# Attention and a gated dense layer on one core: the opening and the main part as one table of steps, laid out anew

## The chip, the cores and the metric

One core of one Trainium2 chip. The metric is the device time of one execution in microseconds (us), as the median of several runs. The engines by the profile's names: PE (TensorE: matmuls; PEld are its weight loads), DVE (VectorE), ACT (ScalarE), POOL (GpSimd, which here also issues all loads) and SP (SyncE, which issues the stores).

## The reference

```python
scores = scale * np.matmul(q, k.transpose(0, 1, 3, 2)) - np.log(S)
attn = 1.0 / (1.0 + np.exp(-scores))
x = np.matmul(attn, v)              # then to [3584, 768]
h = x @ w_in
g = h * (1.0 / (1.0 + np.exp(-beta * h)))
return g @ w_out
```

q, k and v are 8 batches x 12 heads x 448 tokens x 64; w_in is 768 x 2048, w_out 2048 x 768, beta has one value for each of the 2048 columns. Inputs and output are float32.

## The kernel before, in words

All matmuls take fp16 operands; loads cast while they transfer (POOL's queue). Work goes by batches of 448 tokens (8), groups of four heads (24, three to a batch, numbered through) and slots of two heads. Output tiles have 128 tokens (28).

One group goes through these steps. `transpose` (L194, DVE, step R) turns q or k of a group. `visit` (L243, V g.jt) computes a part of the scores by matmuls on 32 rows of PE (L221) and evicts them with a sigmoid on ACT (`weigh`, L230, tile attnT). `attend` (L282, A g) multiplies by v on tiles of 128 rows and 64 columns (L294), the last part of the keys on 64 rows, and DVE casts the result into xT (L303).

The dense layers come next. All of their matmuls go through `dense` (L171): either one matmul with 128 columns of weights, or two of 64 columns beside each other, as `tiled["cols"]` says. For the first batch, and some columns of the second, `dense1` (L308, step D) is the plain product with w_in, a sigmoid on ACT (L320) and a product on DVE (L323) into gt; `dense2` (L341, step O) is the plain product with w_out. All later batches use a Strassen-Winograd scheme with 7 products in place of 8: `wino1` (I b.d.p) and `wino2` (U tile.p.part), with sums of weights (S, T), of tokens (X) and of hidden values (H), which DVE adds (`add`, L375); the second halves of the gating are `weigh_right` (L495, G) and `weigh_below` (L505, B) on POOL.

Matmul results go to one-bank tiles of PSUM from `bank()` (L89), which takes the one used longest ago; scores have two-bank tiles of their own. `share_psum` (L76) lays PSUM out anew once, when the opening's first part is through, and `scores_done` (L634) once the last visit is through.

Sizes of pools that matter: outp has 4 buffers ("osb", 128 x 896 floats). They hold some early attnT tiles, then the scratch a and b of each wino1 block, and the output tiles until `store` (L593, DMA issue at L605, SP's queue) has written them. rawp has 3 buffers for q and k as loaded; xTp has 3.

Every engine works in the order in which the program issues. That order is written out by hand: `STEPS` (L653 to L709) is a list of steps such as `V3.1` or `I2.3.2`, and `follow` (L641) runs them one by one. For each step it looks up which comes next, a V or an A (L646): if it is an A, dense matmuls ahead run as two of 64 columns (L648), else as one of 128.

Ahead of `STEPS`, the opening is plain code (L779 to L834). It computes the first three groups by halves of the tokens, 224 each: `half_visit` (L259), `attend` with 224 columns, and `first_half` (L610), which takes the next of sixteen half `dense1` steps. `idle_units` (L740) are matmuls on zeros that fill time at the start. The loads of q, k, v, w_in (`load_w_in`, L154, eight parts) and w_out (`load_w_out`, L161, four parts) are issued in this code too, all on POOL's queue. In the opening `tiled["cols"]` is 128 throughout. Here is its end:

```python
        firsts.close()
        share_psum(ctx, seconds, 2, N_ONE, 2)
        first_half(4)
        half_visit(1, QH, 0)
        first_half(3)
        half_visit(1, QH, 1)
        transpose(2, 0, NH, NB)
        attend(0, QH, QH)
        ...
        attend(2, QH, QH)
        first_half(1)
        follow(STEPS)
```

Of the kernel before, what the change touches and what calls it, by code (L numbers as in the profile page):

```python
# [13 lines left out]
def kernel(  # L14
# [638 lines left out]
    STEPS = """  # L653
        R3.1 R3.0 D0.6 D0.12 R4.1 D0.14 D0.7 V3.1 R4.0 D0.13 D0.0 D0.8 V3.0 D0.3 D0.9 V3.3 D0.1
        D0.10 E1 D0.2 Q6 V3.2 D0.4 O0.0.0 D0.5 O0.0.1 O0.0.2 V4.1 O1.0.0 O0.0.3 A3 V4.0 O1.0.1 R5.1
        D0.11 D0.15 O0.0.4 R5.0 V4.2 O0.0.5 S1.1 O0.0.6 O1.0.2 O1.0.3 S1.0 O0.0.7 S2.0 O1.0.4 V4.3
# [8 lines left out]
        I2.0.2 H4.1 I2.0.3 R10.1 X2.2 U4.1.0 V9.0 X2.3 U4.1.1 Q11 G2.0 U4.6.0 U4.6.1 Q12 A9 V10.0
        I2.0.7 H4.3 U4.5.0 U4.7.0 U4.5.1 V10.1 U4.7.1 I2.0.4 B2.0.1 U4.3.0 U4.4.0 U4.2.0 B2.0.0
        U4.2.1 R11.0 U4.3.1 U4.4.1 R11.1 I2.1.1 V10.2 Q13 Q14 I2.1.6 I2.1.5 I2.1.7 I2.1.2 K4 I2.1.3
        V10.3 I2.1.4 G2.1 B2.1.0 R12.1 I2.2.1 B2.1.1 A10 V11.0 I2.2.6 I2.2.5 R12.0 I2.2.7 I2.2.2
        I2.2.3 I2.3.1 Q15 G2.2 V11.1 I2.3.6 I2.2.4 B2.2.1 B2.2.0 I2.3.5 I2.3.2 R13.1 I2.3.7 I2.3.3
        V11.2 I2.3.4 B2.3.1 U6.1.0 B2.3.0 H6.2 U6.1.1 A11 H6.0 V12.2 U6.2.0 U6.7.0 H6.1 U6.2.1 G2.3  # L670
# [24 lines left out]
        I6.0.4 H18.3 U18.5.0 G6.0 U18.2.0 R23.0 U18.5.1 U18.2.1 B6.0.1 B6.0.0 U18.7.1 V22.3 U18.3.0
        U18.3.1 U18.4.0 U18.4.1 I6.1.1 I6.1.6 A22 V23.0 I6.1.5 I6.1.7 I6.1.2 I6.1.3 I6.2.1 G6.1
        I6.1.4 B6.1.0 I6.2.6 I6.2.5 B6.1.1 I6.2.2 V23.1 I6.2.7 I6.2.3 I6.3.1 I6.2.4 I6.3.6 G6.2
        B6.2.1 I6.3.5 B6.2.0 I6.3.7 I6.3.2 I6.3.3 V23.2 I6.3.4 B6.3.1 U20.1.0 H20.2 U20.1.1 A23
        U20.7.0 B6.3.0 U22.1.0 H20.0 U20.2.0 H20.1 X7.0 U20.2.1 U20.5.0 U20.6.0 G6.3 U20.6.1 I7.0.1
        U20.5.1 H20.3 X7.2 U22.1.1 U20.7.1 I7.0.2 X7.1 U20.3.0 U20.3.1 U22.2.0 U22.2.1 H22.0 U20.4.0  # L700
        X7.3 H22.2 H22.1 U20.4.1 U22.5.0 I7.0.6 I7.0.5 U22.7.0 I7.0.7 I7.0.3 U22.6.0 G7.0 I7.0.4
        I7.1.1 I7.1.6 I7.1.5 B7.0.0 B7.0.1 I7.1.2 I7.1.7 I7.2.1 I7.1.3 I7.2.6 G7.1 I7.1.4 I7.2.5
        I7.2.7 B7.1.0 B7.1.1 U22.6.1 I7.2.2 I7.2.3 U22.5.1 H22.3 I7.2.4 I7.3.1 I7.3.6 B7.2.0 I7.3.5
        G7.2 B7.2.1 I7.3.7 U22.7.1 I7.3.2 I7.3.3 U24.1.0 I7.3.4 U22.3.0 U22.3.1 U24.1.1 U22.4.0
        B7.3.0 U22.4.1 U24.2.0 B7.3.1 H24.0 U26.1.0 U24.2.1 H24.1 U24.5.0 G7.3 U24.6.0 H24.2 U24.6.1
        U24.5.1 H24.3 H26.0 U24.7.0 U24.7.1 U26.1.1 U24.3.0 U24.3.1 H26.1 U24.4.0 U26.2.1 U26.5.0
        U26.6.0 H26.2 U26.6.1 U26.5.1 H26.3 U26.7.0 U26.7.1 U24.4.1 U26.3.0 U26.3.1 U26.4.0 U26.4.1
        U26.2.0
# [7 lines left out]
    with tc.manual_schedule():  # L716
# [62 lines left out]
        for g in range(1, QPB):  # L779
            load_one(g, 0, 0, NH)  # L780
            load_one(g, 1)
        load_v(0)
# [1 line left out]
        for g in range(QPB - 1):
            load_one(g, 0, NH, NB)
        for c in range(WCH):
            if c == WCH // 2:
                load_one(QPB - 1, 0, NH, NB)
            load_w_in(c)
        for g in range(1, QPB):  # L790
            transpose(g, 0, 0, NH)
            transpose(g, 1)

        for n in range(2 * QPB):
            half_visit(n // 2, 0, n % 2)
            idle_units((3, 4, 4, 4, 2, 2)[n])
        double_v_last(0)
        transpose(0, 0, NH, NB)
        attend(0, 0, QH)
        half_visit(0, QH, 0)  # L800
        attend(1, 0, QH)
        half_visit(0, QH, 1)
        for g in range(1, QPB - 1):
            transpose(g, 0, NH, NB)
        attend(2, 0, QH, (0,))
        attend(2, 0, QH, (1,))
        for i in range(P // BLK):
            part = slice(i * BLK, (i + 1) * BLK)
# [57 lines left out]
```

## Time and profile before

| what | value |
|---|---|
| runs | 368.91, 369.24, 913.54 us; median 369.24 |
| span of the profiled execution | 367.57 us (page: 367.6) |
| median less span | 1.67 us |
| TensorE busy | 361.6 us, 3677 matmuls |
| granted clock of TensorE | 0.99 to 1.00 over the stretches of the span |
| chain by line | matmuls of `dense` 71%, scores 12%, values 10%, stores 2% |

The chain is followed back from the last instruction to what released each; its shares are of the span. In the busy time by stretch each engine has its busy us and, in brackets, its instructions. In the timeline and the chain the first number is the start in us from the span's start, the second the length; neighbours of one kind stand together with their number (x16). A name such as `m_ps<-xT,w_in 128*64 128x224` means: written tile, read tiles, tile of PE (rows*columns), size of the operand.

### The profile page before, as it was taken

What the parts mean: (1) busy time and instruction counts of PE and PEld (TensorE: products, weight loads), DVE (VectorE), ACT (ScalarE), POOL (GpSimd) and SP (SyncE); (2) the same over time, 40 slices, a digit from 0 to 9 for tenths busy, and PEclk for the clock granted to TensorE, in tenths of its full rate; (3) what the DMA queues carried; (4) which work ended last, traced back from release to release, by engine and by line L of the source; (5) the groups of instructions that cost most, each with busy time, mean ns of one, the idle gap of its engine ahead of it and who ended that gap; (6) DMA issues with size and microseconds to landing.
All of it is one profiled execution on the core that took longest, in us unless ns stands there. A gap on an engine that the chain in (4) does not pass through costs nothing.

```text
span 367.6 us, 9130 instructions
## 1 busy us (share of the span) xinstructions
PE 361.6 (98%) x3677; PEld 237.7 (65%) x3677; DVE 272.2 (74%) x524; ACT 248.7 (68%) x410; POOL 154.3 (42%) x192
## 2 busy tenths in 40 slices
PE   8999999999999999999999999999999999999996
PEld 3478754457465685557757667666856688689763
DVE  4356569889995796876778678868879677778764
ACT  5987976789765797657865579977874859225410
POOL 7834523504413873117761445841630316216610
PEclk9999999999999999999999999999999999999999
DMA  8999999930363890517909363373303030030233
GB/s 163 182 197 201 197 206 199 237 40 2 50 139 52 165 147 2 81 57 122 143 9 153 52 137 51 50 79 88 52 1 88 2 87 2 0 87 0 61 67 134
DMA packets 42698, 34.76 MB, mean 95 GB/s; under 512 B 21904, under 2 KB 39200, under 8 KB 42656
## 3 DMA queue, kind: packets, MB, share of 16 engines
q0 software_dynamic: 36688, 22.47, 44.7%
q1 hardware_dynamic: 5968, 11.71, 11.5%
q8 instruction: 29, 0.48, 0.6%
q14 instruction: 13, 0.11, 0.1%
HBM read 45.62 MB, written 11.01 MB: 154 GB/s over the span
## 4 chain that ended last, share of the span: by engine, by line
PE 94%; DMA 3%; ACT 1%; DVE 1%; SPq 0%; issue 0%; ACTq 0%; DVEq 0%
PE m_ps L174 71%; PE sco L221 12%; PE av_ps L294 10%; DMA out_dram<-osb 2%; PE idle_ps L743 1%; ACT attnT L233 1%; DMA gt<-in_k_dram 1%; DVE osb L375 0%; SPq L605 0%; ACT osb L428 0%; DVE xT L303 0%; ACT osb L466 0%; DVE raw L760 0%; SPq L726 0%; DVE kT L763 0%
## 5 line engine op out<-in xcount | busy, mean ns | idle before, releaser
L233 ACT ACTIVATE attnT<-sco 128x896 f16<-128x896 f32 (+1 forms) x163 | 139.2, 908 | 38.5 <-PE sco L221 37.9
L375 DVE TENSOR_TENSOR osb<-m_ps,osb 128x448 f32<-128x448 f32 (+2 forms) x197 | 116.3, 596 | 51.7 <-PE m_ps L174 42.2
L174 PEld LDWEIGHTS <-w_in 128*128 128x128 f16 (+1 forms) x948 | 81.0, 100 | 19.4 <-issue 11.5
L174 PE MATMUL m_ps<-xT,w_in 128*128 128x224 f16 (+3 forms) x750 | 85.5, 266 | 0.8 <-ACT osb L466 0.5
L495 POOL TENSOR_TENSOR gt<-osb,sg 128x448 f16<-128x448 f32 x26 | 29.5, 1135 | 118.4 <-ACT sg L428 108.2
L505 POOL TENSOR_TENSOR gt<-osb,sg 128x448 f16<-128x448 f32 x52 | 58.3, 1137 | 34.9 <-ACT sg L428 33.2
L428 ACT ACTIVATE sg<-osb,beta_sb 128x224 f32<-128x224 f32 (+1 forms) x104 | 54.0, 575 | 10.0 <-DVE osb L375 9.8
L174 PEld LDWEIGHTS <-sum 128*128 128x128 f16 (+1 forms) x444 | 39.9, 99 | 27.4 <-issue 3.7
L174 PEld LDWEIGHTS <-gt 128*128 128x128 f16 (+1 forms) x474 | 36.9, 102 | 25.8 <-issue 7.7
L174 PE MATMUL m_ps<-w_out,gt 128*128 128x384 f16 (+2 forms) x350 | 52.6, 324 | 0.0
L221 PE MATMUL sco<-qT,kT 32*128 32x448 f16 (+3 forms) x864 | 51.4, 340 | 0.4 <-DVE kT L763 0.2
L174 PEld LDWEIGHTS <-w_S 128*128 128x128 f16 (+1 forms) x486 | 43.9, 99 | 7.0 <-issue 6.0
L174 PE MATMUL m_ps<-w_out,sum 128*128 128x384 f16 (+1 forms) x228 | 40.6, 327 | 0.0
L174 PE MATMUL m_ps<-w_T,sum 128*128 128x384 f16 (+1 forms) x216 | 40.3, 326 | 0.0
L303 DVE CAST xT<-av_ps 128x448 f16<-128x448 f32 (+1 forms) x54 | 28.4, 566 | 14.3 <-PE av_ps L294 14.1
L294 PE MATMUL av_ps<-attnT,v 128*64 128x448 f16 (+3 forms) x400 | 38.2, 343 | 0.0
L174 PE MATMUL m_ps<-xs,w_S 128*128 128x224 f16 (+1 forms) x330 | 36.2, 259 | 0.0
L294 PEld LDWEIGHTS <-v 128*64 128x64 f16 (+1 forms) x432 | 20.5, 108 | 18.1 <-issue 10.2
L428 ACT ACTIVATE osb<-m_ps,beta_sb 128x224 f32<-128x224 f32 x52 | 20.4, 449 | 15.3 <-PE m_ps L174 13.8
L221 PEld LDWEIGHTS <-kT 32*128 32x128 f16 (+1 forms) x864 | 13.4, 96 | 23.1 <-issue 20.9
L466 ACT COPY osb<-m_ps 128x448 f32<-128x448 f32 x26 | 13.8, 536 | 18.4 <-PE m_ps L174 15.4
L135 POOL DMA_DIRECT2D v<-in_v_dram x32 | 19.9, 633 | 13.3 <-DMA w_out<-in_moe_w_out_dram 6.5
(53 smaller groups left out, 300.5 us busy)
## 6 DMA issues: line engine op xcount, KB each, us to landing
out_dram<-osb SPq DMA_DIRECT2D x100, 96.0 KB, 2.6
raw<-in_k_dram POOLq DMA_DIRECT2D x23, 224.0 KB, 5.8
raw<-in_q_dram POOLq DMA_DIRECT2D x21, 224.0 KB, 4.5
v<-in_v_dram POOLq DMA_DIRECT2D x32, 144.0 KB, 7.4
w_in<-in_moe_w_in_dram POOLq DMA_DIRECT2D x8, 384.0 KB, 10.4
w_out<-in_moe_w_out_dram POOLq DMA_DIRECT2D x4, 768.0 KB, 13.1
v<-in_v_dram POOLq DMA_DIRECT2D x16, 48.0 KB, 6.2
out_dram<-osb SPq DMA_DIRECT2D x4, 192.0 KB, 2.6
```

The costliest lines, as they stand in the source:

```text
L135: queue.dma_start(out=to[i * BLK : (i + 1) * BLK, h0:h1, 0:JF].rearrange("p h j d -> p h (j d)"), in_=rows[:, :, JF * i * D : JF * (i + 1) ...
L174: nc.tensor.matmul(to[c : c + step], hidden[:, c : c + step], weights, **({} if step == P else {"tile_position": (0, c)}), **flags,)
L221: nc.tensor.matmul(sco[base : base + nk, hh, u0 : u0 + n], kT[g][lo : lo + BLK, jt * P : jt * P + nk, e], qT[g][lo : lo + BLK, c0 : c0 + n ...
L233: nc.scalar.activation(out=at[:, :, 0:n], in_=sco[:, :, 0:n], func=AF.Sigmoid, bias=NEG_LOG_S, scale=MSCALE,)
L294: nc.tensor.matmul(av[hh * D : (hh + 1) * D, 0:n], vs[b][base : base + nk, 2 * (s % NPAIR) + hh, jt], at[base : base + nk, hh, 0:n], start ...
L303: nc.vector.tensor_copy(out=xTs[b][:, s % NPAIR, c0 : c0 + n], in_=av[:, 0:n])
L375: nc.vector.tensor_tensor(out=out, in0=in0, in1=in1, op=op)
L428: nc.scalar.activation(out=out, in_=in_, func=AF.Sigmoid, bias=0.0, scale=beta_sb[:, dc : dc + 1])
L466: nc.scalar.copy(out=oa[:, 0], in_=m)
L495: nc.gpsimd.tensor_tensor(out=gt[:, 2 * d : 2 * d + 2, off : off + QH], in0=ob[:, 0], in1=sg, op=ALU.mult)
L505: nc.gpsimd.tensor_tensor(out=gt[:, dc, off : off + S].rearrange("p (h n) -> p h n", h=2), in0=oa[:, :, j], in1=sg, op=ALU.mult,)
L743: nc.tensor.matmul(idle[:, 0:cols], still[:, 0:P], still[:, 0:cols], start=True, stop=True)
```

## The change

The opening becomes a second table, OPENING, in the same notation, with new letters for its steps, and `follow(OPENING + STEPS)` runs both as one list. `follow` now also counts the half visits (h) and half attends (a) as what comes next, so dense steps ahead of a half attend run as two of 64 columns too. Both tables are laid out anew: the order of the steps is another one from the opening to the end. Among others, three half dense steps (f8, f15, f13) stand behind the first step of STEPS; the second part of w_out's right half (o1.1) is issued there; the beta transposes (b0) come in the midst of the first half visits; h1.0.1 stands ahead of h1.0.0; S1.0 moves into the opening; the load K2 moves behind Q7, Q8 and Q11. Which steps there are stays the same.

```diff
-    todo = list(range(NDC))
-
-    def first_half(n: int):
-        for _ in range(n):
-            dense1(0, todo.pop(0), 0, QH)
+    def load_part(g: int, r: int, half: int):
+        load_one(g, r, half * NH, (half + 1) * NH)
+
+    def turn_beta():
+        for i in range(P // BLK):
+            part = slice(i * BLK, (i + 1) * BLK)
+            nc.vector.transpose(out=beta_sb[part], in_=beta_in[:, part])
+
+    def share_anew():
+        firsts.close()
+        share_psum(ctx, seconds, 2, N_ONE, 2)
...
+        "i": lambda n: idle_units(n),
+        "h": lambda g, half, second: half_visit(g, half * QH, second),
+        "a": lambda g, half, *part: attend(g, half * QH, QH, part or (0, 1)),
+        "f": lambda dc: dense1(0, dc, 0, QH),
+        "r": lambda g, half: transpose(g, 0, half * NH, (half + 1) * NH),
+        "b": lambda _: turn_beta(),
+        "p": lambda _: share_anew(),
+        "l": load_part,
+        "k": lambda g: load_one(g, 1),
+        "v": load_v,
+        "w": load_w_in,
+        "o": load_w_out,
...
-            nearer[i] = nxt if nxt in "VA" else nearer[i + 1]
+            nearer[i] = nxt if nxt in "VAha" else nearer[i + 1]
...
-            tiled["cols"] = D if then == "A" else P
+            tiled["cols"] = D if then in ("A", "a") else P
...
-        R3.1 R3.0 D0.6 D0.12 R4.1 D0.14 D0.7 V3.1 R4.0 D0.13 D0.0 D0.8 V3.0 D0.3 D0.9 V3.3 D0.1
...
+        R3.0 f8 R3.1 f15 f13 o1.1 D0.2 D0.0 V3.0 D0.6 Q6 D0.12 V3.3 f7 f14 R4.1 D0.5 V3.1
+        D0.4 D0.10 R4.0 D0.9 D0.14 S1.1 V3.2 D0.13 D0.11 E1 D0.7 O0.0.0 S2.1 V4.1 O0.0.1
...
+        V5.2 O1.1.4 R6.1 R6.0 X1.0 Q7 O1.1.5 O1.1.6 O1.1.7 Q8 A5 V6.0 X1.1 R8.0 R7.1 D1.3
+        D1.10 T2.0 D1.8 R7.0 V6.2 D1.11 S3.1 Q11 D1.2 K2 V6.1 D1.0 O0.1.7 D1.1 E2 D1.9 V6.3
...
+        U4.5.0 B2.0.0 U4.5.1 I2.1.2 R11.1 I2.1.5 V10.2 U4.3.0 I2.1.3 Q13 U4.7.0 U4.7.1
+        U4.3.1 V10.3 I2.1.7 G2.1 A10 V11.0 I2.1.4 I2.2.1 I2.2.6 U4.4.0 I2.2.5 U4.4.1 B2.1.0
+        B2.1.1 I2.2.2 R13.0 I2.2.3 I2.3.1 R12.1 V11.1 I2.2.7 R13.1 I2.3.2 I2.3.6 R12.0
+        I2.3.5 G2.2 I2.2.4 I2.3.7 B2.2.0 V11.2 B2.2.1 I2.3.3 U6.1.0 E4 I2.3.4 U6.1.1 B2.3.0
...
-        U26.6.0 H26.2 U26.6.1 U26.5.1 H26.3 U26.7.0 U26.7.1 U24.4.1 U26.3.0 U26.3.1 U26.4.0 U26.4.1
-        U26.2.0
+        U26.2.0 U24.3.1 U26.6.1 H26.2 U26.5.0 H26.3 U24.4.1 U26.5.1 U26.7.0 U22.4.1 U26.7.1
+        U26.3.0 U26.3.1 U26.4.0 U26.4.1 U26.2.1
+    """.split()
+
+    OPENING = """
+        l1.0.0 h0.0.0 i4 h0.0.1 k1 l2.0.0 k2 v0 i4 r1.0 R1.1 l0.0.1 h1.0.1 l1.0.1 i2 w0 b0
+        w1 i2 h1.0.0 w2 r2.0 R2.1 i3 w3 h2.0.0 i4 E0 l2.0.1 h2.0.1 w4 r0.1 a0.0 h0.1.0 a1.0
+        h0.1.1 r1.1 a2.0.1 a2.0.0 h1.1.0 p0 w5 f3 w6 w7 f0 f1 Q3 Q4 K1 o0.0 f2 h1.1.1 r2.1
+        f4 o1.0 f6 a0.1 h2.1.0 f5 Q5 f9 a1.1 o0.1 S1.0 h2.1.1 f10 f11 a2.1 f12 D0.1 D0.3
+        D0.8
     """.split()
...
-        firsts.close()
-        share_psum(ctx, seconds, 2, N_ONE, 2)
-        first_half(4)
...
-        follow(STEPS)
+        follow(OPENING + STEPS)
```

More of the change, by code (lines that the diff above doesn't have):

```diff
@@ L665 @@
[L665 to L670, printed above, removed]
@@ L695 @@
[L695 to L700, printed above, removed]
@@ L701 @@
[L701 to L706, printed above, removed]
@@ new lines @@
+        I2.3.5 G2.2 I2.2.4 I2.3.7 B2.2.0 V11.2 B2.2.1 I2.3.3 U6.1.0 E4 I2.3.4 U6.1.1 B2.3.0
+        H6.2 X3.0 B2.3.1 A11 R15.0 G2.3 V12.2 I3.0.1 Q17 X3.1 U6.2.0 U6.7.0 H6.0 H6.1 U6.2.1
+        V12.1 I3.0.6 I3.0.2 U6.6.0 R15.1 U6.6.1 U6.5.0 H6.3 X3.2 U6.5.1 V12.0 X3.3 U6.7.1
+        Q18 U6.3.0 K5 U6.3.1 I3.0.5 U6.4.0 U8.1.0 U6.4.1 I3.0.3 V12.3 H8.2 H8.0 U8.1.1 A12
+        Q14 V13.1 I3.0.7 R18.1 U8.2.0 H8.1 U8.5.0 I3.0.4 U8.7.0 V13.2 U8.6.0 U8.6.1 B3.0.1
+        H8.3 U8.5.1 B3.0.0 U8.7.1 U8.2.1 V13.0 R14.1 R14.0 U8.3.0 U8.3.1 U8.4.0 U8.4.1
@@ new lines @@
+        I3.1.1 G3.0 I3.1.6 A13 V14.1 I3.2.1 I3.1.5 R18.0 I3.1.7 I3.1.2 Q16 I3.1.3 V14.2
+        I3.1.4 G3.1 I3.2.2 I3.2.6 I3.2.5 V14.3 I3.2.7 I3.2.3 I3.3.1 G3.2 I3.2.4 B3.2.0
+        B3.1.1 B3.1.0 I3.3.6 I3.3.5 I3.3.2 I3.3.7 E5 B3.2.1 I3.3.3 U10.1.0 V14.0 I3.3.4
+        B3.3.1 X4.0 B3.3.0 H10.2 U10.1.1 Q19 I4.0.1 G3.3 A14 V15.2 U10.2.0 X4.1 X4.2 U10.7.0
+        U10.2.1 H10.0 H10.1 R16.1 I4.0.6 R16.0 X4.3 V15.0 U10.6.0 I4.0.2 K6 U10.6.1 U10.5.0
+        V16.1 I4.0.5 U10.5.1 U10.7.1 H10.3 V15.1 I4.0.3 U10.4.0 U10.3.0 U10.3.1 U10.4.1
@@ new lines @@
+        H12.0 I4.0.7 A15 V16.2 Q20 U12.1.0 H12.1 I4.0.4 U12.1.1 B4.0.0 U12.6.0 I4.1.1 R17.0
+        I4.1.6 U12.6.1 G4.0 H12.2 V16.0 U12.2.0 B4.0.1 I4.1.5 E6 U12.2.1 H12.3 R17.1 U12.5.0
+        I4.1.2 I4.1.3 G4.1 U12.5.1 I4.1.7 U12.7.0 U12.7.1 U12.3.0 I4.2.1 I4.1.4 U12.3.1
+        U12.4.0 V16.3 R20.0 U12.4.1 Q22 B4.1.0 A16 V17.2 I4.2.6 I4.2.5 I4.2.2 I4.2.7 V17.1
+        R19.1 I4.2.3 I4.2.4 G4.2 I4.3.1 I4.3.6 V17.0 I4.3.5 I4.3.7 B4.2.0 I4.3.2 I4.3.3
+        B4.2.1 V18.2 I4.3.4 B4.1.1 X5.0 I5.0.1 R20.1 A17 V18.0 U14.1.0 X5.1 U14.1.1 X5.2
@@ new lines @@
+        I5.0.6 R19.0 B4.3.1 B4.3.0 Q21 V18.1 U14.2.0 I5.0.5 G4.3 I5.0.7 X5.3 I5.0.2 I5.0.3
+        V18.3 G5.0 H14.0 U14.2.1 I5.0.4 H14.1 A18 V19.2 U14.5.0 B5.0.0 B5.0.1 I5.1.1 U14.6.0
+        H14.2 K7 I5.1.6 U14.6.1 R21.0 U14.5.1 V19.0 U14.7.0 I5.1.5 H14.3 U14.7.1 I5.1.2
+        I5.1.3 U14.3.0 V19.1 G5.1 U14.3.1 I5.1.7 U14.4.0 V20.0 U14.4.1 R21.1 I5.2.1 I5.1.4
+        A19 B5.1.1 V20.2 I5.2.6 I5.3.1 I5.2.5 Q23 I5.2.7 E7 I5.2.2 I5.2.3 V20.1 I5.2.4
+        B5.1.0 I5.3.6 B5.2.0 I5.3.5 I5.3.7 R23.0 B5.2.1 G5.2 I5.3.2 I5.3.3 V20.3 I5.3.4
@@ new lines @@
+        U16.1.0 U16.1.1 B5.3.1 B5.3.0 H16.2 R23.1 A20 V21.2 U16.2.0 X6.0 U16.7.0 U16.2.1
+        H16.0 R22.1 G5.3 I6.0.1 U16.5.0 H16.1 V21.0 U16.6.0 X6.2 U16.6.1 H16.3 I6.0.2
+        U16.5.1 X6.1 R22.0 U16.7.1 V21.1 H18.0 U16.3.0 I6.0.6 U16.3.1 U16.4.0 H18.1 U16.4.1
+        V22.1 X6.3 I6.0.5 A21 V22.0 I6.0.3 U18.6.0 U18.1.0 U18.5.0 U18.1.1 V22.2 U18.6.1
+        I6.0.7 H18.3 U18.5.1 U18.2.0 I6.0.4 U18.2.1 V22.3 H18.2 G6.0 U18.3.0 A22 B6.0.1
+        V23.0 U18.7.0 B6.0.0 U18.7.1 U18.3.1 I6.1.1 I6.1.6 U18.4.0 I6.1.5 U18.4.1 I6.1.7
@@ new lines @@
+        I6.1.2 I6.1.3 I6.1.4 G6.1 I6.2.1 B6.1.1 V23.2 B6.1.0 I6.2.6 I6.2.5 I6.2.2 I6.2.7
+        I6.2.3 I6.3.1 V23.1 I6.3.6 G6.2 I6.3.2 I6.2.4 I6.3.5 I6.3.7 U20.1.0 U20.1.1 I6.3.3
+        H20.2 B6.2.1 I6.3.4 B6.2.0 G6.3 A23 X7.0 U20.2.0 X7.1 B6.3.1 B6.3.0 U20.2.1 X7.3
+        H20.0 I7.0.1 U22.1.0 H20.1 X7.2 I7.0.6 U20.7.0 I7.0.5 I7.0.2 U20.5.0 U20.6.0 U20.6.1
+        H20.3 U20.5.1 U20.7.1 I7.0.3 I7.0.7 G7.0 U20.3.0 U20.3.1 U22.1.1 I7.0.4 U20.4.0
+        I7.2.1 I7.2.6 H22.0 U20.4.1 B7.0.0 I7.1.1 I7.2.5 B7.0.1 I7.2.2 H22.1 I7.2.7 I7.2.3
@@ new lines @@
+        I7.1.6 U22.5.0 I7.2.4 I7.1.5 G7.2 I7.1.7 I7.3.1 B7.2.0 U22.6.0 I7.3.6 I7.1.2 I7.1.3
+        B7.2.1 I7.1.4 I7.3.5 H22.2 B7.1.1 U22.2.0 U22.6.1 I7.3.2 I7.3.7 G7.1 U22.7.0 I7.3.3
+        B7.1.0 H22.3 I7.3.4 B7.3.1 U22.5.1 U24.1.0 H24.2 U24.1.1 B7.3.0 U22.2.1 U22.7.1
+        U22.3.0 U22.3.1 H24.0 U24.2.0 U26.1.0 U24.7.0 H24.1 U24.5.0 U24.6.0 G7.3 U24.6.1
+        H24.3 U24.5.1 H26.0 U24.2.1 U24.7.1 H26.1 U22.4.0 U26.1.1 U24.3.0 U26.6.0 U24.4.0
+        U26.2.0 U24.3.1 U26.6.1 H26.2 U26.5.0 H26.3 U24.4.1 U26.5.1 U26.7.0 U22.4.1 U26.7.1
@@ L778 @@
         nc.vector.transpose(out=words[:, JF * P :], in_=raw[:, 1, NF * D :].bitcast(FP32))
[L779 to L782, printed above, removed]
         nc.sync.dma_start(out=beta_in[0:NDC], in_=moe_beta.rearrange("(c p) -> c p", p=P))
[L784 to L808, printed above, removed]
-            nc.vector.transpose(out=beta_sb[part], in_=beta_in[:, part])
-        load_qk(QPB)
-        load_qk(QPB + 1)
-        load_v(1)
-        load_w_out(0, 0)
-        load_w_out(1, 0)
-        load_qk(QPB + 2)
-        load_w_out(0, 1)
-        load_w_out(1, 1)
-        firsts.close()
-        share_psum(ctx, seconds, 2, N_ONE, 2)
-        first_half(4)
-        half_visit(1, QH, 0)
-        first_half(3)
-        half_visit(1, QH, 1)
-        transpose(2, 0, NH, NB)
-        attend(0, QH, QH)
-        first_half(1)
-        half_visit(2, QH, 0)
-        first_half(4)
-        half_visit(2, QH, 1)
-        attend(1, QH, QH)
-        first_half(3)
-        attend(2, QH, QH)
-        first_half(1)
-        follow(STEPS)
+        follow(OPENING + STEPS)
 _INS = ['q', 'k', 'v', 'moe_w_in', 'moe_w_out', 'moe_beta']
```

44 lines of the change are left out of this document (10 added, 34 removed).

## The prediction, on record before the changed kernel ran

> **What bounds the kernel now.** I read the page's first part, then the chain, then the busy time by stretch, and last the timeline of TensorE where the edit lies.
>
> ```profile
> span 367.6 us, 9130 instructions
> PE 361.6 (98%) x3677; PEld 237.7 (65%) x3677; DVE 272.2 (74%) x524; ACT 248.7 (68%) x410; POOL 154.3 (42%) x192
> PE 94%; DMA 3%; ACT 1%; DVE 1%; SPq 0%; issue 0%; ACTq 0%; DVEq 0%
> ```
>
> TensorE is busy for 361.6 of 367.6 us, and the chain that ended last runs over it for 94% of the span. Only 6 us are not matmul time. The busy time by stretch says where they lie (second number of each row):
>
> ```profile
> core 0: us, PE busy (x) PEld busy (x) DVE busy (x) ACT busy (x) POOL busy (x), PEclk, DMA share, GB/s
> 0.00:20.00 20.00, 18.16 (x212) 8.11 (x213) 8.45 (x28) 14.37 (x20) 15.26 (x27) 1.00 1.20 175
> 20.00:45.00 25.00, 25.00 (x320) 19.56 (x318) 15.35 (x44) 21.87 (x43) 11.27 (x18) 1.00 1.40 198
> 170.00:185.00 15.00, 14.38 (x168) 12.46 (x168) 11.99 (x21) 12.09 (x23) 10.96 (x14) 1.00 0.96 148
> 312.00:367.60 55.60, 52.03 (x402) 37.84 (x396) 38.88 (x70) 16.05 (x35) 16.53 (x15) 0.99 0.22 58
> ```
>
> The first 20 us lose 1.84 (start, first loads), the last stretch 3.57 (the last add and the last store), 170 to 185 loses 0.62. The granted clock is full throughout. From 20 to 170 us, and in the stretches that I leave out, TensorE has no gap. So an edit gains only if TensorE's own instructions take less time, or if it removes the one wait in the middle. That wait is in the chain, in order of time:
>
> ```profile
> 171.48 5.85 DMA out_dram<-osb
> 177.51 0.66 ACT osb L428 x2
> 178.19 1.72 ACT attnT L233 x2
> 179.91 0.43 ACT osb L466
> 180.37 0.64 DVE osb L375
> ...
> 181.77 0.73 PE m_ps L174 x6
> ```
>
> A store that landed late (5.85 us, with loads of K and Q in flight) kept a buffer of the pool outp; ACT waited 1.23 us for it, its later evictions came late, and the matmuls started 0.95 us later than their rows without a gap would (0.71 at 180.4, 0.24 at 181.8).
>
> **The change, part by part.** The amount of matmul work is the same: as many D, O, I, U, V and A steps, the same halves f, 19 idle matmuls in both. What differs is the order, and how many dense matmuls run as two of 64 columns.
>
> *Two of 64 columns.* What does such a pair cost, and what does a change of tile shape cost? The timeline of TensorE answers both:
>
> ```profile
> 29.96 0.99 PE L294 MATMUL av_ps<-attnT,v 128*64 128x224 f16 x16
> 30.88 1.90 PE L174 MATMUL m_ps<-xT,w_in 128*128 128x224 f16 x18
> 32.71 0.98 PE L294 MATMUL av_ps<-attnT,v 128*64 128x224 f16 x16
> 125.14 0.77 PE L174 MATMUL m_ps<-xs,w_in 128*64 128x224 f16 x12
> 125.73 0.74 PE L174 MATMUL m_ps<-xT,w_in 128*64 128x224 f16 x12
> 126.31 1.61 PE L294 MATMUL av_ps<-attnT,v 128*64 128x448 f16 x16
> 133.01 0.74 PE L174 MATMUL m_ps<-xs,w_in 128*128 128x224 f16 x6
> 133.59 0.74 PE L174 MATMUL m_ps<-xs,w_S 128*128 128x224 f16 x6
> ```
>
> From start to start, 6 whole matmuls take 0.58 us (133.01 to 133.59), 0.096 each. 18 of them ahead of an attend take 1.83 (30.88 to 32.71): 18 x 0.096 = 1.73, and 0.10 more for the change from 128 to 64 columns. The 12 halves at 125.73 take 0.58 as well, and the attend behind them starts with no extra. So a pair costs what one whole matmul costs, and the change ahead of the attend goes. By medians over the trace a change costs 0.097 us. Counted in the order of the two programs, neighbours on TensorE of different tile shape go from 216 to 209: -7 x 0.097 = **-0.68 us**. Five of the seven lie ahead of the fourth group's first visit, where the opening's attends now have halves on both sides or scores directly behind them; two lie later, from the new order. Halves behind scores start 0.02 late (125.14 to 125.73 is 0.59, not 0.57 to 0.58); some three more such entries give **+0.07**. Bounds: -0.90 if the entries were free and the dearer kinds of change go, 0 if what follows waits for something else.
>
> The Trainium skill, "TensorEngine Tiling (Array Packing)", section Restrictions, says that column tiling turns off Fast Weight Load; by that the added pairs could pay for slower loads. The trace has no sign of it: six pairs take 0.59 us and six whole matmuls 0.58.
>
> *What can use those 0.5 us in the opening.* Visit V3.0 needs group 3's q and k; k is issued at 21.03 on POOL's queue and, by the list of transfers of that moment, lands 13.4 us later, at 34.4:
>
> ```profile
> 21.03 0.54 POOL L115 DMA_DIRECT2D raw<-in_k_dram  x1 [1.15 <-DMA w_in<-in_moe_w_in_dram]
> ```
>
> ```profile
> raw<-in_k_dram POOLq DMA_DIRECT2D x1, 224.0 KB, 13.4
> ```
>
> The transposes then take 0.63 for q (landed at 33.75) and 0.57 for k, in DVE's order q first, so V3.0 can start at about 35.4. Before, its first weights load at 36.61. In the new table one half dense (0.58) less lies ahead of it and five changes (0.49) go: 36.61 - 1.07 = 35.54. It just fits. But R3.0 now stands ahead of f8's eviction on DVE: while it waits for the q that lands at 33.75, up to 0.65 us, that eviction and the next sit behind it, and TensorE needs the bank. I take **+0.1**, bounds 0 and 0.65.
>
> *Weights' first use and sums.* The loads keep their order up to w_out on POOL's queue; only K2 moves behind Q7, Q8 and Q11. The parts of w_in land at 16.7 to 31.4, and by counted matmul time each first use in the new order comes 0.1 to 0.5 us behind its landing: nothing, at worst 0.3. K2, by the rows of issue and landing near it, would land near 72 where it is needed at about 76: nothing. T3.0 stands where w_out's last part lands (58.03), some 1.4 to 2 us after DVE gets there; evictions queue behind it on DVE. By DVE's rows it catches up before TensorE runs out of banks: nothing, bounds 0 and 1. The beta transposes now come early on DVE, where DVE is busy 8.45 of 20 us: nothing; their absence later likewise.
>
> *The wait at 177.5.* The tables differ from the first step to the last, so the place no longer exists as such. Output buffers are shared by four tiles; the distance in matmul time from a tile's last dense to the next write of its buffer was at least 7.2 us before, 7.9 at the place that waited. In the new order the shortest are 3.6, 5.8, 6.1 and 6.7. A store undisturbed is away 4.6 to 5.8 us after that dense, 10.3 at the place that waited. The shortest (U4.4.1 to I2.3.2, about 126 us) makes ACT wait 1.0 to 2.2 us, but ACT's next urgent work, V11.2's sigmoid, comes some 4 us later: nothing on TensorE, at most 1.7. So of the 0.95 I take half as saved: **-0.5**, bounds -0.95 and +1.7.
>
> *The end.* The last stores come from steps U26 as before, but U22.4.1 (a tile over four DMAs) moves to 3.9 us before the last matmul ends. SP takes 0.43 us for one such DMA by its rows near 346 us (two in 0.78, three in 1.40) and 0.64 where stores collide (eight in 5.14). At 0.43 SP is free again before the last add is through; at 0.64 the last store is issued 0.9 late. I take **+0.1**, bounds 0 and 0.9.
>
> **Sum.** The profiled execution has a span of 367.57 and the median run 369.24; the 1.67 around the span is taken as unchanged. 367.57 - 0.68 + 0.07 + 0.10 - 0.5 + 0.1 = 366.7 of span, **368.3 us** as a run. With all helpful bounds 367.57 - 0.90 - 0.95 + 1.67 = 367.4. More can't come off, since the matmul work stays and it is 98% of the span: that rules out a gain of 2% (7.4 us), which is about what a measurement of this kernel can tell from no change.
>
> **The rivals.**
>
> *The gain is swallowed (the switching changes nothing).* The 0.49 us of the opening are earned ahead of V3.0. If q and k land 0.5 later than before, or if R3.0 holds the evictions behind it for the whole 0.65, V3.0 starts at 36.0 to 36.2 in place of 35.54. For it: k was in the air for 13.4 us with DMA share at 1.40 in that stretch, and the landing sets the start to within 0.1. Against it: the loads ahead of it are the same and in the same order. The sum then loses 0.46 to 0.66 and keeps the rest: 368.8 to 369.0, and up to 369.4 with the bound of the sums of w_out in part.
>
> *Slower: the output buffers bind.* Place: the reuses at 5.8 to 6.7 us. If one such store meets loads as at 171.48 and is away only after 10.3 us, ACT is 3.6 to 4.5 us late there, and TensorE, at 0.95 lost for 1.23 of ACT's wait, 2.8 to 3.5. One such place, or the shortest one at its bound of 1.7 together with the old wait's half kept, turns the sign: it decides from 0.9 us of loss on TensorE. Time: 368.3 + 1.7 = 370.0 to 368.3 + 3.2 = 371.5, middle 370.8. For it: four distances shorter than any before, and the one wait that before has is of this kind. Against it: by the order on POOL's queue few of the new short reuses have loads right beside them.
>
> *The weight loads show.* The order has 90 more pairs with 224 columns of tokens and 16 fewer of other sizes, net 74. If the two loads of a pair (0.11 us each in the rows of the attends' own weights) were paid in full in place of 0.096, each would cost 0.12 more: 74 x 0.12 = 8.9, so 377. The 220 pairs of before run at the whole matmul's pace, which leaves this little. It is what the Trainium skill's rule named above would lead to, and the trace disagrees.
>
> **How the numbers follow.** Forecast 0.47, with its own range 367.5 to 368.8; gain swallowed 0.22, 368.8 to 369.4; buffers 0.28, 369.4 to 371.6; weight loads 0.03. The predicted time is the likeliest case's, 368.3. Range 367.3 to 371.0: it takes in the first two cases and two thirds of the third. Faster by over 2% needs 7.4 us off work that is the same: 0.01. Slower by over 2% (above 376.6) would need the weight loads or three colliding stores: 0.05. Within 2%: 0.94.
>
> **What would show it.** Right: TensorE's busy time falls by some 0.6 to 360.9 or 361; halves of f sit ahead of each attend of the opening as 128*64 with no extra start to start; V3.0's first weights load near 35.5; in the list of waits, ACT on the store of osb stays under 2.5 us in all, and 170 to 185 is full; the last store is issued 0.4 us behind the last matmul. Wrong: V3.0 at 36 or later with DVE waiting for raw; a stretch between 85 and 312 where TensorE is under 99% busy with a DMA of osb as the releaser; SP issuing back to back up to the end; pairs that take more than 0.10 each.

## The result, and the profile after

The changed kernel takes 384.74 us in the median (381.80 to 386.81) against 369.08 before: a ratio of 1.043, 95% interval 1.037 to 1.049. It is slower by 4.3%, outside the predicted range of 367.3 to 371.0. The profiled execution has a span of 385.0 us. One of the four runs of the kernel before took 913.54 us and doesn't enter the ratio.

The page's totals and the shares of the chain, after:

```profile
span 385.0 us, 9275 instructions
PE 367.4 (95%) x3751; PEld 240.3 (62%) x3751; DVE 285.9 (74%) x524; ACT 248.9 (65%) x410; POOL 159.6 (41%) x192
PE 80%; DVE 11%; DMA 4%; issue 1%; ACT 1%; SPq 1%; POOL 1%; DVEq 0%; POOLq 0%
```

TensorE is idle for 17.6 us in place of 6.0, and busy for 367.4 in place of 361.6. DVE, 1% of the chain before, is 11% now. And DVE is busy for 285.9 us in place of 272.2 with the same 524 instructions: that is the line to stop at. The busy time by stretch, columns as before:

```profile
20.00:45.00 25.00, 24.84 (x351) 20.66 (x350) 15.67 (x43) 22.19 (x44) 11.58 (x18) 1.00 1.40 199
45.00:85.00 40.00, 40.00 (x394) 21.24 (x391) 31.77 (x60) 29.95 (x43) 11.09 (x20) 1.00 1.10 171
85.00:130.00 45.00, 40.50 (x389) 24.37 (x382) 35.47 (x59) 28.93 (x45) 19.54 (x23) 0.96 0.47 75
130.00:170.00 40.00, 37.44 (x364) 24.25 (x361) 31.18 (x57) 24.71 (x40) 17.72 (x21) 0.96 0.53 92
200.00:230.00 30.00, 27.68 (x252) 17.74 (x250) 22.92 (x39) 14.60 (x24) 12.24 (x16) 0.94 0.57 83
320.00:385.00 65.00, 58.83 (x508) 43.33 (x504) 47.71 (x80) 21.46 (x45) 22.09 (x19) 1.00 0.19 50
```

From 20 to 85 us TensorE loses 0.16 us, at 30.4. Behind that are gaps, in three stretches with a granted clock of 0.94 to 0.96. What TensorE waited for (us in total, times, longest), from the list of waits:

```profile
PE m_ps L174 <- DVE sum L375: 4.3, 3, 2.3
PE m_ps L174 <- DVE osb L570: 4.1, 2, 2.4
PE m_ps L174 <- DVE xs L375: 1.7, 1, 1.7
PE m_ps L174 <- DVE xT L303: 1.2, 2, 0.8
```

There are two stories in it. The copies at L570 waited for an output buffer; in the chain, in order of time, around 166 us:

```profile
159.47 6.04 DMA out_dram<-osb
...
165.63 0.57 DVE osb L570
...
166.24 0.94 PE m_ps L174 x3
```

The copy empties the bank of P1 into an output tile. The tile's buffer was in a store for 6.04 us, and P2 (U8.2.0) goes into that same bank, so TensorE stood for 1.72 us; at 115.3, ahead of U4.2.0, for 2.40.

Nearly all others behind 85 us were waits for DVE's own work. The chain ahead of the longest of them, 2.32 us at 203.1:

```profile
195.40 1.63 DVE sum L375
197.03 0.47 DVE osb L570
197.50 1.07 DVE xT L303 x2
198.59 0.90 DVE xs L375
199.49 2.25 DVE xT L375
201.75 0.61 DVE sum L375
202.38 0.70 DVE sum L375
203.13 3.05 PE m_ps L174 x14
```

Here H10.2 (sum) takes 1.63 us and H10.0 and H10.1 0.61 and 0.70; X4.1 (xs) 0.90 and X4.2 (xT) 2.25 (2.33 from its own start, at 199.41), where an X takes 0.50. The same operations, by form, first in the kernel before, then after (columns: busy us, mean ns):

```profile
L375 DVE TENSOR_TENSOR sum<-gt 128x1024 f16<-128x1024 f16 x26 | 17.9, 688 | 1.4 <-POOL gt L505 1.2
L375 DVE TENSOR_TENSOR xs<-xT 128x672 f16<-128x672 f16 x7 | 3.5, 498 | 0.0
L375 DVE TENSOR_TENSOR xT<-xT 128x672 f16<-128x672 f16 x7 | 3.5, 495 | 0.0
L505 POOL TENSOR_TENSOR gt<-osb,sg 128x448 f16<-128x448 f32 x52 | 58.3, 1137 | 34.9 <-ACT sg L428 33.2 <-PE sco L221 1.4 <-PE m_ps L174 0.3
```

```profile
L375 DVE TENSOR_TENSOR sum<-gt 128x1024 f16<-128x1024 f16 x26 | 21.1, 814 | 0.8 <-POOL gt L505 0.6
L375 DVE TENSOR_TENSOR xs<-xT 128x672 f16<-128x672 f16 x7 | 6.2, 881 | 0.0
L375 DVE TENSOR_TENSOR xT<-xT 128x672 f16<-128x672 f16 x7 | 6.3, 896 | 0.0
L505 POOL TENSOR_TENSOR gt<-osb,sg 128x448 f16<-128x448 f32 x52 | 62.9, 1224 | 76.5 <-ACT sg L428 70.6 <-PE m_ps L174 5.6 <-POOL gt L505 0.2
```

Adds whose two operands both lie in SBUF have become slower, and POOL's products too; adds with one operand in PSUM have not (621 ns in both). Held against POOL's timeline one by one: of the 96 such adds, 21 start while a product is running, and 19 of these are stretched, by 0.04 to 0.95 us, the more the more of the product is left (the other two start in its last 0.14 us). During 11 more a product starts; 10 of these aren't stretched (there the product is the longer one, up to 1.6 us), and X4.2 is, by 1.8. The other 64 are within 0.02 us of their duration before. Together this is 13.9 us, all of DVE's increase. In the kernel before one add starts beside a running product and is 0.11 longer. The order is what keeps them apart there: B3.1.0 and B3.1.1 stood right behind G3.1, while in the new table they come behind B3.2.0, and seven products stand nearly in a row from 190.6 to 199.1, where H10 and X4 follow.

### The profile page after: what moved, and what is told of

Its sections match the earlier page's. It is cut to its first block, busy times and chain, and to the rows that moved or that the text cites. A ratio compares the mean times of both kernels' runs of the same rounds, so it can differ in the third digit from the quotient of the medians.

```text
span 385.0 us, 9275 instructions
## 1 busy us (share of the span) xinstructions
PE 367.4 (95%) x3751; PEld 240.3 (62%) x3751; DVE 285.9 (74%) x524; ACT 248.9 (65%) x410; POOL 159.6 (41%) x192
## 3 DMA queue, kind: packets, MB, share of 16 engines
q1 hardware_dynamic: 5968, 11.71, 11.6%
## 4 chain that ended last, share of the span: by engine, by line
PE 80%; DVE 11%; DMA 4%; issue 1%; ACT 1%; SPq 1%; POOL 1%; DVEq 0%; POOLq 0%
PE m_ps L174 62%; PE sco L221 10%; PE av_ps L294 7%; DMA out_dram<-osb 3%; DVE sum L375 2%; DVE osb L375 2%; DVE xT L303 1%; DVE xs L375 1%; PE idle_ps L774 1%; DMA gt<-in_k_dram 1%; SPq L605 1%; POOL gt L505 1%; DVE osb L570 1%; DVE xT L375 1%; DVE w_in L375 0%
## 5 line engine op out<-in xcount | busy, mean ns | idle before, releaser
L505 POOL TENSOR_TENSOR gt<-osb,sg 128x448 f16<-128x448 f32 x52 | 62.9, 1224 | 76.5 <-ACT sg L428 70.6
L174 PE MATMUL m_ps<-xT,w_in 128*128 128x224 f16 (+2 forms) x798 | 85.6, 266 | 0.4 <-ACT osb L466 0.2
L495 POOL TENSOR_TENSOR gt<-osb,sg 128x448 f16<-128x448 f32 x26 | 30.3, 1165 | 86.4 <-ACT sg L428 81.4
L428 ACT ACTIVATE sg<-osb,beta_sb 128x448 f32<-128x448 f32 (+1 forms) x104 | 54.8, 575 | 14.5 <-DVE osb L375 14.5
L174 PE MATMUL m_ps<-w_out,gt 128*128 128x384 f16 (+2 forms) x340 | 54.5, 329 | 4.5 <-DVE osb L570 4.1
L174 PE MATMUL m_ps<-w_T,sum 128*128 128x384 f16 (+1 forms) x212 | 41.7, 331 | 3.2 <-DVE sum L375 2.3
L174 PE MATMUL m_ps<-w_out,sum 128*128 128x384 f16 (+1 forms) x228 | 42.5, 334 | 2.2 <-DVE sum L375 2.0
L294 PE MATMUL av_ps<-attnT,v 128*64 128x448 f16 (+3 forms) x400 | 39.4, 349 | 0.0
L294 PEld LDWEIGHTS <-v 128*64 128x64 f16 (+1 forms) x432 | 21.6, 110 | 17.3 <-issue 9.2
L115 POOL DMA_DIRECT2D raw<-in_q_dram x26 | 15.1, 582 | 26.5 <-DVE qT L199 16.6
L323 DVE TENSOR_TENSOR gt<-m_ps,sg 128x224 f16<-128x224 f32 (+1 forms) x40 | 16.5, 433 | 12.5 <-ACT sg L320 12.2
## 6 DMA issues: line engine op xcount, KB each, us to landing
w_in<-in_moe_w_in_dram POOLq DMA_DIRECT2D x8, 384.0 KB, 10.6
```

The costliest lines, as they stand in the source:

```text
L115: nc.gpsimd.dma_start(out=raws[g][:, r, c0:c1].rearrange("p c d -> p (c d)"), in_=(q, k)[r][b, HQ * t : HQ * (t + 1)].rearrange("h (p c) d ...
L174: nc.tensor.matmul(to[c : c + step], hidden[:, c : c + step], weights, **({} if step == P else {"tile_position": (0, c)}), **flags,)
L294: nc.tensor.matmul(av[hh * D : (hh + 1) * D, 0:n], vs[b][base : base + nk, 2 * (s % NPAIR) + hh, jt], at[base : base + nk, hh, 0:n], start ...
L323: nc.vector.tensor_tensor(out=gt[:, dc, off : off + n], in0=m1[:, 0:n], in1=sg[:, 0:n], op=ALU.mult)
L428: nc.scalar.activation(out=out, in_=in_, func=AF.Sigmoid, bias=0.0, scale=beta_sb[:, dc : dc + 1])
L495: nc.gpsimd.tensor_tensor(out=gt[:, 2 * d : 2 * d + 2, off : off + QH], in0=ob[:, 0], in1=sg, op=ALU.mult)
```

## The experiments

The theories: **P**, a DVE add of two SBUF operands is held while POOL works on a product. **S**, stores that are slow beside loads hold the output buffers. **C**, the gaps cost clock on top. The rivals: DVE late by its order alone; the opening at fault; reuse too early whatever the loads do.

**The opening alone.**

```diff
 OPENING: ... f9 a1.1 o0.1 h2.1.1 f10 f11 a2.1 f12 f8 o1.1 f15 f13 f7 f14
 STEPS:   as before the change
```

> The new opening in its table, with halves ahead of its attends, then the old main table (S1.0, D0.1, D0.3, D0.8 stay in the main table; f8, o1.1, f15, f13, f7, f14 end the opening). If the loss lies in the new main table and the opening's tile changes are worth what the prediction says: 368.6, from 368.2 to 369.1. Rival (the new opening is itself part of the loss): 370 or more.

Measured: 368.31 against 368.58 of the kernel before on the same chip, ratio 0.9989 (0.9978 to 0.9999). So the loss is in the main table. The 0.1% isn't shown to be the opening's: in this profile the fourth group's first visit starts at 37.12, later than the 36.61 of before, since TensorE waits for a part of w_in:

```profile
32.41 4.77 PE L174 MATMUL m_ps<-xT,w_in 128*128 128x224 f16 x48 [0.62 <-DMA w_in<-in_moe_w_in_dram]
```

What is shorter lies behind it: the stretch from 170 to 185 is full, without the 0.95 us that the kernel before lost there.

**POOL's products cut short in the changed kernel, and in the kernel before.**

```diff
+        w = QH if b == 1 else 1
 ...
-            in0=ob[:, 0], in1=sg
+            in0=ob[:, 0, :, 0:w], in1=sg[:, :, 0:w]
```

> The changed kernel with POOL's products (steps G and B) of batches 2 to 7 cut to the first column of each block, so that their gating is left out; the first gated batch keeps them whole; all waits and the order stay. Theory P (a DVE add with two operands in SBUF is held while POOL works on a product): behind 100 us the stretched adds return to 0.68 and 0.50 us, DVE's busy time falls by about 11 us to 275, TensorE's waits on DVE sums at 148.9, 203.1, 331.5 and 365.1 (5.7 us in all) go with the half clock behind 203 (1.7): 384.7 - 7.4 = about 377; the waits behind the copies at L570 and the one at 95.8 stay. Rival (the order on DVE is late by itself): more than half of the 5.7 us stays, 381 or more.

> The kernel before with the same cut of POOL's products of batches 2 to 7 to one column (their gating left out). Theory P: one add of 96 is stretched there, by 0.11 us, so nothing is to be had: 368.6, within 0.7. Rival (shorter products help for another reason, such as earlier values for TensorE): 2 us or more faster.

Measured: 374.16 in place of 384.74, and 369.46 against 368.52 for the kernel before (ratio 1.002, 1.001 to 1.003). The page of the changed kernel cut so (span 372.6), and what its TensorE waited for:

```profile
PE 362.5 (97%) x3751; PEld 238.5 (64%) x3751; DVE 274.4 (74%) x524; ACT 249.0 (67%) x410; POOL 91.8 (25%) x192
```

```profile
PE m_ps L174 <- DVE osb L575: 2.2, 2, 1.8
...
PE m_ps L174 <- DVE sum L375: 1.1, 1, 1.1
```

DVE is at 274.4 and TensorE's waits for it behind 100 us are gone: those of 148.9, 203.1, 331.5 and 365.1. What stays for sums, 1.1 us at 95.8, is in the first gated batch, whose products are whole. The gain of 10.6 is above the 7.4 expected for two reasons: the granted clock was 1.00 throughout, and the waits behind the copies fell from 4.1 to 2.2 us though no load was moved in the table. The kernel before gains nothing. P holds and the rival falls: DVE's order is not late without the stretching. What this cut can't tell apart is POOL being free earlier from DVE not being held; the next pair can.

**More work on POOL in the kernel before: reading, and only writing.**

```diff
+        nc.gpsimd.tensor_tensor(out=sg, in0=oa[:, :, j], in1=sg, op=ALU.mult)   # first kernel
+        for _ in range(2):
+            nc.gpsimd.memset(sg, 0.0)                                            # second kernel
```

> The kernel before with each product on POOL made twice, the second time back into the sigmoid's tile that nobody reads; the output is the same work. POOL's products go from 88.6 to about 177 us. Theory P: with POOL reading SBUF over half of the time behind 100 us, a third or more of the adds of two SBUF operands there are stretched; DVE's busy time rises from 272 by 10 us or more, TensorE waits on DVE, 375 or more. Rival (POOL's lateness alone costs): DVE's busy time stays within 3 us of 272.

> The kernel before with two memsets of the same sigmoid's tile behind each product, in place of the second product: POOL is late in a similar way but reads nothing more. Theory P (it is POOL's reads that hold DVE's second operand): DVE's busy time stays within 3 us of 272, and the time is several us below that of e9_twice. Rival (any work on POOL holds DVE): DVE's busy time rises as in e9_twice, in proportion to POOL's.

Measured: 420.8 and 404.5. Both are far slower, since TensorE then also waits for POOL's late values; the times alone prove little, and the expectation that DVE's total would stay within 3 us of 272 failed for the memsets (278.9, against 288.0 for the doubled products), as the later products now ran beside other adds. With the doubled products 23 of the 96 adds start during a product and 21 are stretched, fewer than the third that was expected. The single instructions decide. In the kernel with memsets, around 149 us:

```profile
148.30 0.69 DVE L375 TENSOR_TENSOR sum<-gt 128x1024 f16<-128x1024 f16 x1 [6.05 <-POOL gt L507]
148.33 1.00 POOL L514 MEMSET sg<- 128x448 f32 x2
149.03 0.69 DVE L375 TENSOR_TENSOR sum<-sum,gt 128x1024 f16<-128x1024 f16 x1
...
149.29 1.41 POOL L495 TENSOR_TENSOR gt<-osb,sg 128x448 f16<-128x448 f32 x1
149.64 1.43 DVE L375 TENSOR_TENSOR xs<-xT 128x672 f16<-128x672 f16 x1
```

Beside two memsets a sum takes its 0.69. A product that starts during the second sum takes 1.41 in place of 1.14, and the xs behind it 1.43 in place of 0.50. Over the whole run, the 12 adds that have only memsets beside them are stretched by 0.01 at most; the 8 that start during a product by 0.70 on average. One more, a sum at 192.25, behind whose start a product begins, is 1.25 longer, as X4.2 was.

**Loads moved away from the stores in the changed kernel.** First K4 behind B2.0.0 and K5 behind B3.0.0:

> The changed kernel with two loads moved in the table and nothing else: K4 behind B2.0.0 and K5 behind B3.0.0, so that neither is in flight when the stores of tiles 2 and 3 (issued at 106.8 to 109.2) and of tiles 6 and 7 (about 159) are. Theory S (stores late beside loads hold output buffers, and the copy that waits for the buffer holds the PSUM bank): the waits of TensorE behind the copy at L570, 2.40 us at 115.3 and 1.72 at 166.2, shrink to under 0.3 each, and the half clock for about 3.4 us behind each goes too: 4.1 + 2 x 1.7 = 7.5 us less, about 377. Rival (the reuse comes too soon by the order itself, with or without loads): both waits stay over 1.5 us and the time within 1 us of 384.7.

Measured: 384.87, no gain. The two waits are gone, but another has come, at I2.2.2: the copy of I2.2.1 (L466) writes into the buffer of tile 4, with K4 now beside that tile's store, and I2.2.2 goes into the bank that the copy empties:

```profile
134.01 0.53 ACT L466 COPY osb<-m_ps 128x448 f32<-128x448 f32 x1 [4.18 <-DMA out_dram<-osb]
134.59 0.74 PE L174 MATMUL m_ps<-xT,w_in 128*128 128x224 f16 x6 [2.81 <-ACT osb L466]
```

Then K4 later still, behind B2.2.0, with E4 behind U8.1.1:

> The changed kernel with K4 behind B2.2.0, its copy E4 behind U8.1.1, and K5 behind B3.0.0. In the run with K4 behind B2.0.0 the two waits behind L570 went, and a new one of 2.81 us came at 134.6, behind an ACT copy that waited for a store, beside K4's transfer. Theory S: with K4 clear of that place as well, all three are under 0.5 us, and 4.1 us of waits and two spells of half clock (3.4 us) go: 377.2. Rival (some store waits wherever the order is this tight): one or more of 1.5 us stays, 380 or more.

Measured: 382.36. All three waits are under 0.5 us, but DVE's stretched adds now come to matter at 147.5 (1.65) and 149.8 (0.95), where TensorE had been late before. The first add ahead of them isn't P's: it has no product beside it, only POOL's issuing of K4's loads, and takes 1.45 in place of 0.50:

```profile
140.08 2.51 POOL L135 DMA_DIRECT2D v<-in_v_dram  x4
141.88 1.45 DVE L375 TENSOR_TENSOR xs<-xT 128x672 f16<-128x672 f16 x1
```

The next, at 144.88, is 2.10 longer beside three products in a row. In the changed kernel 21 adds stood beside load issues without being longer, so what makes the difference here stays open. At the same mean clock (0.999) the span is 379.7 against 380.0 of the changed kernel: nearly all of the gain was given back to longer adds. S is right about the places and their cause, and its price can't be read off with the longer adds still there.

**Both taken away.** The loads as in the last kernel, the products one column in all batches:

> The changed kernel with both suspected costs taken away: the products on POOL cut to one column in all batches (their gating left out; a memset of the cells concerned while POOL waits at about 65 us), and the loads K4, K5 and the copy E4 moved as in the run e5_loads. Theory P and S together: the products cut alone gave 374.2, with 2.2 us of waits behind stores and 2.0 us of waits in the first gated batch left; without these 374.2 - 4.2 = 370.0 or less, down to the 368.3 that was predicted. Rival (something else in the new order costs too): 372 or more, with waits of TensorE that neither theory names.

Measured: 370.61 (369.08 to 372.72), ratio 1.0057 (1.004 to 1.008); the profiled execution, with a span of 367.3, is the shortest of them:

```profile
PE 361.2 (98%) x3751; PEld 238.2 (65%) x3751; DVE 272.0 (74%) x524; ACT 248.4 (68%) x410; POOL 88.4 (24%) x194
```

TensorE's and DVE's busy times are those of before, and the longest wait left behind 20 us is 0.63. The median lies between the 370.0 of the theories and the 372 of the rival. P and S with what follows from them account for the loss up to 1.7 us of the median, which no run explains; the runs of this kernel lie up to 3.6 us apart.

**Three steps moved, all work kept.**

```diff
 STEPS: G3.3 behind X4.3, G5.3 behind X6.2, G7.3 behind H24.3
```

> The changed kernel with all its work and three steps moved, so that POOL's products don't stand beside the adds that follow: G3.3 behind X4.3, G5.3 behind X6.2, G7.3 behind H24.3. Theory P: X4.2 (2.33 us), X6.2 (1.44) and H24.0 (1.60) fall to 0.50, 0.50 and 0.68; TensorE's wait of 2.32 at 203.1 falls under 0.7 and that of 0.92 at 365.1 under 0.4; 2 us less at equal clock, and without the half clock behind 203 a median of 381 to 383. Rival (DVE is late there by its own order): the wait at 203 stays over 1.5 us.

Measured: 381.40 (381.16 to 382.41). X4.2 and X6.2 take 0.50 and 0.49, and TensorE's wait for H10 is 0.49 in place of 2.32:

```profile
197.02 0.50 DVE L375 TENSOR_TENSOR xT<-xT 128x672 f16<-128x672 f16 x1
...
198.90 0.82 PE L174 MATMUL m_ps<-w_T,sum 128*128 128x384 f16 x4 [0.49 <-DVE sum L375]
```

H24.0 stayed at 1.60 and its wait at 0.93: the product beside it is still G7.3. No other step of POOL or ACT stood between its old place and its new one, so it started as before, at 357.99, 0.08 us ahead of H24.0. Moving a step in the table helps only where that makes the product start later: G3.3 now waits for a sigmoid that stands behind others on ACT. Two other adds came beside products (0.84 and 0.50 longer), and DVE's busy time fell only from 285.9 to 284.2. At a like clock the spans are 379.5 and 380.0: most of the 3.3 us between the medians is clock, and 0.5 is left where 2 were expected.

**Idle matmuls put into the three longest gaps.**

> The changed kernel with matmuls that nobody reads put into its three longest waits: 8 of 512 columns ahead of U4.2.0 (wait 2.40 us) and of U10.6.0 (2.32), 5 ahead of U8.2.0 (1.72); 0.216 us each, so 1.73, 1.73 and 1.08. Nothing else is done. Theory C (a gap of TensorE of about 1.7 us or more brings half the clock for 3.4 us): the granted clock stays at 1.00 in all stretches behind 10 us, TensorE's waits shrink by what was filled, and the time falls by 3 x 1.7 = 5.1 to about 379.7, in all runs alike. Rival (the clock falls for another reason, or the fillers delay what they stand ahead of): 384 or more.

Measured: 387.26. The fillers didn't fill: two of the three groups took a bank that the same late DVE had to empty, so they waited too (2.34 and 2.27 us) and then ran behind the gap; only the one ahead of U10.6.0 ran in time and left a wait of 1.61. The added work is 21 x 0.216 = 4.5 us. But the profile shows something else about C. Busy times behind the gaps, after first, then this kernel:

```profile
115.50:118.90 3.40, 3.40 (x24) 1.97 (x20) 3.34 (x7) 0.86 (x2) 1.14 (x1) 0.53 0.00 0
204.00:207.40 3.40, 3.40 (x18) 1.62 (x16) 1.69 (x4) 0.79 (x2) 2.15 (x4) 0.50 1.44 150
```

```profile
115.80:119.20 3.40, 3.40 (x28) 1.68 (x27) 3.30 (x6) 0.79 (x2) 1.13 (x1) 1.00 0.00 0
204.90:208.30 3.40, 3.40 (x30) 2.05 (x30) 1.38 (x3) 1.03 (x3) 1.85 (x4) 1.00 1.49 147
```

Behind gaps of 2.40 and 2.32 us the clock was half for some 3.4 us (and 0.51 from 166.4 to 169.7, behind that of 1.72); behind gaps of 2.34 and 1.61 it was full. In the kernel with three steps moved it was 1.00 throughout, with gaps of 1.76 and 1.71. The length of the gap alone does not decide. So the price of a spell is shown, and what sets it off isn't. Over the four runs of the changed kernel, 380.0 us of span go with a mean clock of 0.999 and 385.0 with 0.987: up to 5 us of a run are clock.

**Whole matmuls in the opening, and a load moved ahead.**

> The new opening and the old main table as in e4_opening, but with the opening's dense matmuls whole, 128 columns throughout. Changes of tile shape go from 211 to 214. By the prediction's 0.097 us each this is 0.3 slower than e4_opening: 368.6 against 368.3, TensorE's busy time 0.3 up. Rival (pairs of 64 columns cost more than whole matmuls, as the Trainium skill's TensorEngine Tiling (Array Packing), section Restrictions, could be read): it is as fast as e4_opening or faster.

> The new opening and the old main table as in e4_opening (368.3), with the load K5 moved ahead to behind G3.0, so that it is in flight while POOL waited anyhow (158 to 166 us) and not beside the stores of tiles 6 and 7. Theory S for the kernel before: its only wait in the middle, 0.95 us around 178 to 182, is gone or stays gone, 367.5 to 368.3, and TensorE is full from 20 us to the tail. Rival (the wait is due to the order of reuse, not to the load): a wait of ACT or DVE on a store of 0.7 us or more stays.

Measured: 368.81 for the whole matmuls, ratio 1.000 (0.998 to 1.002), beside 0.9989 for the same opening with pairs: not to be told apart. TensorE's busy time is 360.6 with whole matmuls and 361.0 with pairs, where 0.3 more was expected with whole ones. In the traces 12 pairs ahead of an attend take 1.19 (25.48 to 26.67), 12 whole ones 1.25 (25.25 to 26.50); but what the pairs earn there they lose to the wait for w_in, and the fourth group's first visit starts at 37.12 with pairs and 36.43 with whole matmuls. With K5 behind G3.0: 368.17 against 368.88, ratio 0.9976 (0.9963 to 0.9989), all work done; TensorE has no wait from 33 us to the tail. It is the fastest kernel of the study, a quarter of a per cent ahead of the kernel before, with the new opening, the old order and one load moved. What the load adds isn't shown: without it moved the wait around 178 to 182 was already gone, and the ratio was 0.9989 (0.9978 to 0.9999).

## Why the prediction was wrong

- **Tile shapes and the opening: the price fits the changed kernel's trace, and as a gain it isn't shown.** V3.0 began at 35.69 us where 35.54 was worked out. The difference is a wait of 0.16, for a half dense step's eviction on DVE whose sigmoid came late from ACT:

```profile
29.98 0.73 DVE L323 TENSOR_TENSOR gt<-m_ps,sg 128x224 f16<-128x224 f32 x2 [0.15 <-ACT sg L320]
30.43 5.33 PE L174 MATMUL m_ps<-xT,w_in 128*128 128x224 f16 x54 [0.16 <-DVE gt L323]
```

  The sum had 0.1 for R3.0 holding up evictions, but R3.0 ran at 33.71 and TensorE didn't wait there: that the sizes agree is luck. The opening alone gave 0.1% (0.4 us) where about half a microsecond was expected, and by its profile not from its tile shapes.
- **w_in's parts, T3.0, K2, the tail: right as costed.** In the changed kernel TensorE doesn't wait for w_in and is full from 45 to 85 us, and the last gap is 3.4 us where it was 3.5. With the opening alone the wait for w_in was 0.62, above the bound of 0.3.
- **Output buffers: the kind was named, the places and the price were not.** The rival named the reuses at 5.8 to 6.7 us; U4.4.1's was taken as harmless, and it was. The two that bound were the copies of U4.1.1 and U8.1.1, 4.1 us together, above the sum's bound of 1.7; by the trace their buffers came back after 5.2 and 4.4 us of matmul time, less than the rival counted. Distance in matmul time alone was the wrong measure: from the end of U6.3.1 to the end of U8.1.1 there are 4.4 us both in the changed kernel, where the store took 6.04 and TensorE waited, and with K4 and K5 moved, where it didn't.
- **The step that failed** is the sentence that opens the change part by part: "The amount of matmul work is the same", and that what differs is the order. DVE's and POOL's moved steps were costed at nothing, each at its row's duration. Hardly a row of before showed another duration, because the old order put an add beside a running product only once, for 0.25 us. Beside each other they took 13.9 us more of DVE, and 7.7 us of TensorE's waits are waits for it; with both suspected costs taken away 0.2 of these are left.
- **Clock: not in the sum at all.** It was taken as full; three spells of 3.4 us at half, 1.7 lost in each, cost some 5 us of the profiled execution.

So of the 17.4 us of longer span, 11.6 are idle time of TensorE (4.1 from stores, 7.7 from DVE, less a few tenths won) and 5.8 longer busy time, nearly all of it clock.

The Trainium skill has the rule that speaks against this change, and the prediction did not weigh it: SBUF — State Buffer, section Who interferes with whom, says that a DVE instruction with two SBUF inputs contends with a GpSimd instruction that reads SBUF, not with one that only writes it, that the port pair which the two share is an exclusive lock, and that issue order decides who blocks. These runs agree with each part: adds are stretched behind a product and not behind a memset, and the product is stretched where the add came first. The adds that were longer beside load issues aren't explained by it.

## What to carry to other kernels

A duration in a trace is that of the company it ran in: when steps move, ask for each engine pair whether two instructions that never met will meet now, and look in the old trace for the one instance where they did (0.80 us for a sum at 184.3, in place of 0.69). A total busy time that rises with the count of instructions unchanged is the quickest sign of it. And where one resource is relieved, look at who was hidden behind its wait before counting the gain.

## What the runs showed of the hardware

- DVE's add of two SBUF operands waits for a POOL product in progress, up to 0.95 us in the changed kernel; POOL's product waits for the add where that came first (up to 1.6 us in place of 1.14). Memsets on POOL cost the add nothing (at most 0.01 us in 12 cases). DVE's 130 adds of 128x448 with an operand in PSUM took 621 ns each in both kernels.
- Beside POOL's issuing of loads most adds keep their duration (21 in the changed kernel), but an xs took 1.45 in place of 0.50 with nothing else beside it. X4.2's 2.33 us, longer than one product, began during such an issue; why stays open.
- Half the clock for about 3.4 us follows some gaps of TensorE of 1.7 to 2.4 us and not others. The Trainium skill, TensorE: Matmul & The Clock Gate, Part 1, says that an activity window of about 3.4 us, running freely, sets the clock, and that it goes to half after an idle window; the length of the spells agrees, but gaps clearly shorter than a window were enough here.
